# Local and pooled attention with a gated feed-forward: the leftover tokens of all batches as one block of 512, and a newly planned start

## Chip, cores and metric

The kernel runs on one core of a Trainium2 chip. Its engines work side by side, each through its own queue in order: TensorE (PE, matmuls into PSUM), VectorE (DVE), ScalarE (ACT), GpSimd (POOL) and SyncE (SP), which here only issues DMAs. The metric is device time in microseconds (us).

## What is computed

Attention over 8 batches, 8 heads, 576 tokens and 64 features per head is the sum of two parts. One lets every token see its neighbours less than 4 places away; the other averages groups of 4 tokens, attends among the 144 groups, and repeats each result 4 times. The result, 4608 tokens of 512 features, goes through a feed-forward layer with a rational function in its middle. Cut to what matters:

```python
q_d, k_d, v_d = (a.reshape(B, H, S // 4, 4, D).mean(axis=3) for a in (q, k, v))
out_up = np.repeat(sm_attn(q_d, k_d, v_d), 4, axis=2)
mask = np.abs(pos[:, None] - pos[None, :]) < 4
scores = np.where(mask, scale * np.matmul(q, k.transpose(0, 1, 3, 2)), -1e9)
out_local = np.matmul(softmax(scores), v)
x = (out_up + out_local).transpose(0, 2, 1, 3).reshape(B * S, H * D)
h = x @ w_in
P = a[0] + a[1] * h + a[2] * h**2 + a[3] * h**3
Q = 1.0 + abs(b[0]) * abs(h) + abs(b[1]) * h**2
out = (P / (Q + 1e-6)) @ w_out
```

`w_in` is 512 × 2048 and `w_out` 2048 × 512, both given in 64-bit floats.

## The kernel before

**Blocks and steps.** The feed-forward goes over blocks of tokens. The first 512 tokens of a batch are a block; the last 64 tokens (`REST`) of four batches together are a block of 256. `block_plan` orders them 0, 1, 2, R, 3, 4, 5, 6, R', 7. A step fills one PSUM bank of 512 columns with hidden values: one slice of 128 hidden features for a block of 512, two for a block of 256 (`fg`). So a block of 512 has 16 steps, one of 256 has 8: 144 in all. `h_part` issues a step's first product (L695 for block 0, L707 after it), `middle` the rational function on ACT (L720) and DVE (L735 to L771), and `o_part` the second product (L802), two steps behind, into banks 4 to 7.

**Split operands.** From block 1 on, x, the weights and the middle's result are split in a rounded part and a remainder, and a product is three matmuls (`PROD`). `split_x` splits x in place; `weights` turns a chunk of 64-bit weights into 32-bit words (L334 on ACT, L337 and L340 on DVE) and `parts` splits them (L354 on ACT, L357 on DVE). Block 0 uses the unsplit w_in and x.

**Attention.** Four pairs of heads make a batch. Of a pair, PE computes scores (L413, L423) and pooled scores (L440), DVE takes maxima (L455, L485), ACT exponentials (L470, L496), DVE normalizes (L521 for batch 0's pooled part, L531; ACT at L513 for other batches), PE transposes (L544, L551), ACT copies back (L557, L567, L568), PE applies the weights to v (L594, L582), and `put_x` (L626) adds both parts into x. Batch 0 pools q and k on DVE (L401); the others by accumulating DMAs of POOL (L390). The attention of a batch is issued into the steps of the block before it; batch 0's has nothing to run beside, and which PSUM banks its four pairs use is listed in `FIRST`: banks of the scores, of the pooled scores, of the transposes, and of the result.

**Order.** All work is entered as tasks with a cost and, for some, a due time; `Plan.run` sorts them: every engine takes the task that is ready and due earliest, and the program is written out in that order. The constants at the file's end (`H0`, `PARTS_EARLY`, `COEF`, `HOLD`...) shape the due times. The plan's times decide order only; on the chip each engine waits for semaphores.

**Fillers.** In the gaps that the plan leaves on PE at the start, `warm` issues matmuls on constants into bank 7 (L924), whose result nobody reads. They are placed up to the first task of step 0.

Of the kernel before, what the change touches and what calls it, by code (L numbers as in the profile page):

```python
# [182 lines left out]
def attention_moe(  # L183
# [123 lines left out]
    add("DVE", 0.2, lambda: nc.vector.tensor_copy(out=identb.ap, in_=ident.ap), (ident,), (identb,))  # L307
    add("SP", 0.5, lambda: nc.sync.dma_start(out=maskb.ap, in_=mask), (), (maskb,), load=0.5)

# [42 lines left out]
    def parts(w, f, due=None):  # L352
        hi, lo, word = high[w][f], low[w][f], bits[w][f]
        add("ACT", 0.5, lambda: nc.scalar.copy(out=hi.ap, in_=word.ap.bitcast(F32)), (lo,), (hi,), due=due)  # L354
# [19 lines left out]
    def load_qk(c, at=0.0):  # L374
        s, b, i = c.slot, c.b, c.i
        add("SP", 1.46, lambda: nc.sync.dma_start(out=s.qk.ap, in_=qk[b, i]), (), (s.qk,), load=1.46, at=at)

    def load_vw(c, at=0.0, due=None):
        s, b, i = c.slot, c.b, c.i
        add("SP", 0.82, lambda: nc.sync.dma_start(out=s.vw.ap, in_=vw[b, i]), (), (s.vw,), load=0.82, at=at, due=due)  # L380

# [23 lines left out]
    def scores(c, bk):  # L405
# [23 lines left out]

        add("PE", 1.01, issue, (s.qk, identb, maskb), bk)  # L430

    def scores_pooled(cs, bk):
        def issue():
            for i in range(NQ):
                for c, x in zip(cs, bk):
                    pq = flat(c.slot.pq.ap)
                    for j in range(2):
                        js = slice(j * D, (j + 1) * D)
                        o = c.pos(j) * D
                        nc.tensor.matmul(  # L440
                            x.ap[o : o + D, i * SD : (i + 1) * SD],
                            lhsT=pq[js, i * QC : i * QC + D],
                            rhs=pq[js, SD:],
                            start=True, stop=True, skip_group_check=True,
                        )

        add("PE", 1.02, issue, [c.slot.pq for c in cs], bk)

# [55 lines left out]
    def normalize(c):  # L504
# [12 lines left out]

        if c.b in EP_DVE:
            add(
# [17 lines left out]
    def turned(c, bk):  # L537
# [28 lines left out]
        add("PE", 0.11, lambda: turn_local(4, t1.ap[:, NQ * P :]), (s.el, ident), (t1,))  # L566
        add("ACT", 0.49, lambda: nc.scalar.copy(out=s.et.ap[:, :4, :], in_=tp.ap.rearrange("p (c k) -> p c k", k=P)), (tp,), (s.et,))  # L567
        add("ACT", 0.16, lambda: nc.scalar.copy(out=s.et.ap[:, 4, :], in_=t1.ap[:, NQ * P :]), (t1,), (s.et,))  # L568
# [4 lines left out]
    def weighted(cs, bk, due):  # L573
# [38 lines left out]
        def put_x(c, bank, at, lo, hi, cost):  # L612
# [7 lines left out]
            else:  # L620
                xf, r0 = xsf[2][1], c.b % 4 * REST
                dst = xf.ap[:, c.i, r0 : r0 + REST]
                room = part(xf, None, 4 * (c.i * 4 * REST + r0), 4 * REST)
            add(
# [11 lines left out]
        for c, x in zip(cs, avb):  # L636
# [30 lines left out]
    def split_x(k):  # L667
# [3 lines left out]
        for c in range(NCC):  # L671
            hi, lo = (part(x, x.ap[:, c, :], 4 * c * t, 4 * t) for x in blk.x)
            x = xsf[blk.slot][1].ap[:, c, :]
            add("ACT", 0.11 + t / 1390, lambda hi=hi, x=x: nc.scalar.copy(out=hi.ap, in_=x), (lo,), (hi,), due=due)
            add(
# [46 lines left out]
    def middle(n):  # L722
# [120 lines left out]
    for r in range(POOL):  # L843
        v = vf[r // 2]
        if r % 2:
            add(
                "POOL", 0.93, lambda r=r, v=v: nc.gpsimd.dma_start(out=v.ap, in_=vp[0, r], accum_op=ALU.add),
                (v,), (v,), load=1.3,
            )
        else:  # L850
            add("SP", 0.8, lambda r=r, v=v: nc.sync.dma_start(out=v.ap, in_=vp[0, r]), (), (v,), load=0.8)
    for c in c0:
# [37 lines left out]

    attend(1)
    for n in range(NS + LAG):
        if n < NS:
            k, s = steps[n]
# [9 lines left out]
        if o >= 0:  # L904
# [5 lines left out]
            if s == blocks[k].nstep - 1:  # L910
                store(k)

                if blocks[k].b is None and blocks[k - 1].b + 2 < B:
                    attend(blocks[k - 1].b + 2)
                elif blocks[k].b is not None and blocks[k].b + 2 < B and blocks[k + 1].b is not None:
                    attend(blocks[k].b + 2)
        if n < NS:
# [4 lines left out]
    def warm(n):  # L922
        for _ in range(n):
            nc.tensor.matmul(banks[7].ap[:, : 2 * P], lhsT=identb.ap, rhs=flat(maskb.ap)[:, : 2 * P], start=True, stop=True)  # L924
# [35 lines left out]
FIRST = (  # L960
# [70 lines left out]
```

## Time and profile before

| | |
|---|---|
| median of 3 runs | 983.53 us (983.12 to 984.9) |
| the profiled execution | 985.16 us, of which the span from first to last instruction is 983.4 |
| busy: PE, DVE, ACT, POOL | 961.4, 836.5, 811.8, 147.5 us |
| mean granted clock of PE | 0.991 |
| L802, one matmul of 512 columns | 402 ns (wh), 391 (wl) |
| chain that ended last | PE 88%, ACT 7%, DMA 2% of the span |

A matmul's duration overlaps that of the next, so a step's time is read from the chain of work or from a window, not from durations. The views used below are: the windows (busy time of each engine in a stretch of the span, with the count of instructions, the granted clock, the busy share of the DMA engines and GB/s), the chain of work that ended last (start, length, what), the timeline (start, length, engine, line, operation, count, and in brackets how long the engine had been idle and what ended it), the groups by line, and the waits. SPq is SP issuing a DMA; x9 means nine instructions merged into one row.

### The profile page before, as it was taken

To read this page: it belongs to the slowest core of one execution; us is meant where nothing else is said; L and a number is where in the kernel's file an instruction comes from. 1 tells how busy PE (TensorE), PEld (TensorE's weight loads), DVE (VectorE), ACT (ScalarE), POOL (GpSimd) and SP (SyncE) were. 2 spreads that over 40 slices of the span, in tenths; PEclk is the share of its full clock that TensorE was granted. 3 is DMA by queue.
4 is the path that set the end of the run, shared out by engine and by line. 5 is a ranking of instruction groups with operands and counts; after the bars stand their busy time and mean duration, and the time that the engine had idled before them with its cause. 6 is when DMAs were issued, how large, how long until landed. Compare 5 with 4: busy or idle time off the path is not lost.

```text
span 983.4 us, 19740 instructions
## 1 busy us (share of the span) xinstructions
PE 961.4 (98%) x7343; PEld 759.8 (77%) x7343; DVE 836.5 (85%) x1472; ACT 811.8 (83%) x2078; POOL 147.5 (15%) x176
## 2 busy tenths in 40 slices
PE   6999999999999999999999999999999999999997
PEld 4655667778788788988888787878788788898886
DVE  5889999988888888888878887988798888888886
ACT  5789999978889797679797979798888979767775
POOL 1032303031312222002222031303030220000000
PEclk9989999999999999999999999999999999999999
DMA  9577665142333333013333243424242320100001
GB/s 294 192 216 211 166 186 102 68 76 75 64 104 74 77 75 94 1 47 72 78 74 95 72 78 75 76 95 87 69 87 87 65 49 1 44 1 22 1 1 43
DMA packets 46359, 83.43 MB, mean 85 GB/s; under 512 B 6552, under 2 KB 29080, under 8 KB 46264
## 3 DMA queue, kind: packets, MB, share of 16 engines
q1 hardware_dynamic: 25912, 63.00, 19.4%
q0 software_dynamic: 20352, 19.19, 14.1%
q8 instruction: 58, 0.95, 0.4%
q14 instruction: 37, 0.30, 0.1%
HBM read 72.72 MB, written 9.44 MB: 84 GB/s over the span
## 4 chain that ended last, share of the span: by engine, by line
PE 88%; ACT 7%; DMA 2%; DVE 1%; issue 1%; SPq 0%; ACTq 0%; DVEq 0%
PE psum L802 38%; PE psum L707 36%; PE psum L582 2%; PE psum L695 2%; PE psum L594 2%; ACT m L720 2%; PE psum L551 2%; PE psum L544 2%; PE psum L423 1%; PE psum L440 1%; ACT el L470 1%; DMA qk<-in_qk_dram 1%; DMA sl<-in_w_out_dram 1%; ACT gb L720 1%; ACT sl L334 1%
## 5 line engine op out<-in xcount | busy, mean ns | idle before, releaser
L802 PE MATMUL psum<-wh,g 128*128 128x512 f32 x1152 | 369.5, 402 | 0.5 <-issue 0.4
L720 ACT ACTIVATE m<-psum,cf 128x512 f32<-128x512 f32 x288 | 218.0, 757 | 63.1 <-PE psum L707 58.2
L707 PE MATMUL psum<-xs,wh 128*128 128x512 f32 (+1 forms) x1152 | 267.3, 370 | 1.4 <-ACT gb L720 1.4
L802 PEld LDWEIGHTS psum<-wh,g 128*128 128x128 f32 x1152 | 209.4, 188 | 50.1 <-issue 5.5
L707 PEld LDWEIGHTS psum<-xs,wh 128*128 128x128 f32 x1152 | 199.0, 189 | 38.3 <-ACT gb L720 2.0
L802 PE MATMUL psum<-wl,g 128*128 128x512 f32 x576 | 224.5, 391 | 0.0
L720 ACT ACTIVATE gb<-psum,cf 128x512 f32<-128x512 f32 x144 | 116.2, 807 | 55.6 <-PE psum L802 55.6
L390 POOL DMA_DIRECT2D pq<-in_qkp_dram x84 | 73.6, 910 | 485.3 <-DMA pq<-in_qkp_dram 453.5
L707 PE MATMUL psum<-xs,wl 128*128 128x512 f32 (+1 forms) x576 | 142.7, 370 | 0.0
L762 DVE TENSOR_TENSOR g<-m,m 128x512 fp32r<-128x512 f32 x144 | 99.3, 690 | 47.7 <-ACT m L720 46.0
L802 PEld LDWEIGHTS psum<-wl,g 128*128 128x128 f32 x576 | 108.1, 188 | 23.7
L735 DVE SCALAR_TENSOR_TENSOR m<-m,cf,m 128x512 f32<-128x512 f32 x144 | 107.4, 746 | 15.7 <-ACT m L720 15.1
L741 DVE TENSOR_TENSOR m<-m,gb 128x512 f32<-128x512 f32 x144 | 99.1, 688 | 24.0 <-ACT gb L720 20.9
L707 PEld LDWEIGHTS psum<-xs,wl 128*128 128x128 f32 x576 | 100.5, 189 | 18.6 <-issue 1.2
L470 ACT ACTIVATE el<-psum,nm 128x64 f32<-128x64 f32 x320 | 97.3, 348 | 17.6 <-DVE nm L462 17.6
L720 ACT ACTIVATE gb<-m,cf 128x512 f32<-128x512 f32 x144 | 107.9, 749 | 0.7 <-DVE m L735 0.7
L765 DVE SCALAR_TENSOR_TENSOR m<-m,g 128x512 f32<-128x512 f32 x144 | 99.3, 689 | 3.3
L770 DVE TENSOR_TENSOR m<-m,m 128x512 f32<-128x512 f32 x144 | 99.1, 688 | 2.3
L740 DVE TENSOR_TENSOR m<-m,m 128x512 f32<-128x512 f32 x144 | 98.5, 684 | 1.9 <-ACT m L720 1.9
L771 DVE TENSOR_TENSOR g<-m,m 128x512 fp32r<-128x512 f32 x144 | 98.0, 681 | 0.8
L720 ACT ACTIVATE m<-gb 128x512 f32<-128x512 f32 x144 | 93.6, 650 | 3.0
L390 POOL DMA_DIRECT2D vp<-in_vp_dram x84 | 72.3, 945 | 153.9 <-DMA vp<-in_vp_dram 146.8
(63 smaller groups left out, 994.0 us busy)
## 6 DMA issues: line engine op xcount, KB each, us to landing
qk<-in_qk_dram SPq DMA_DIRECT2D x32, 590.0 KB, 6.5
pq<-in_qkp_dram POOLq DMA_DIRECT2D x84, 144.0 KB, 3.3
vw<-in_vw_dram SPq DMA_DIRECT2D x32, 320.0 KB, 3.8
out_dram<-xf SPq DMA_DIRECT2D x32, 256.0 KB, 2.0
sl<-in_w_out_dram SPq DMA_DIRECT2D x15, 512.0 KB, 4.6
sl<-in_w_in_dram SPq DMA_DIRECT2D x12, 512.0 KB, 4.8
vp<-in_vp_dram POOLq DMA_DIRECT2D x84, 72.0 KB, 3.0
pq<-in_qkp_dram SPq DMA_DIRECT2D x28, 144.0 KB, 2.2
```

The lines of the kernel that those rows point to most:

```text
L390: lambda d=dst, x=src, r=r: nc.gpsimd.dma_start(out=d.ap, in_=x[b, r, :, i], accum_op=ALU.add),
L470: nc.scalar.activation(out=s.el.ap[:, k, c.pos(j), :], in_=view[:, j, k, :], func=AF.Exp, bias=nm[:, 5 * j + k : 5 * j + k + 1], scale=sca ...
L707: nc.tensor.matmul(ph.ap[:, f * t : (f + 1) * t], lhsT=(high, low)[j][0][fc].ap[:, c, :], rhs=blk.x[i].ap[:, c, :], start=(part_ == 0 and ...
L720: add("ACT", cost, lambda: nc.scalar.activation(out=out_.ap, in_=in_, func=func, **kw), (room_in, cf, *more), (out_,))
L735: lambda: v.scalar_tensor_tensor(out=tb.ap, in0=tq.ap, scalar=b1, in1=tb.ap, op0=ALU.mult, op1=ALU.add),
L740: add("DVE", 0.61, lambda: v.tensor_tensor(out=ta.ap, in0=ta.ap, in1=tq.ap, op=ALU.mult), (ta, tq), (ta,))
L741: add("DVE", 0.61, lambda: v.tensor_tensor(out=ta.ap, in0=ta.ap, in1=u.ap, op=ALU.add), (ta, u), (ta,))
L762: add("DVE", 0.61, lambda: v.tensor_tensor(out=gh.ap, in0=ta.ap, in1=tq.ap, op=ALU.mult), (ta, tq), (gh,))
L765: lambda: v.scalar_tensor_tensor(out=tb.ap, in0=tb.ap, scalar=CONE, in1=gh.ap.bitcast(F32), op0=ALU.add, op1=ALU.mult),
L770: add("DVE", 0.61, lambda: v.tensor_tensor(out=tb.ap, in0=ta.ap, in1=tb.ap, op=ALU.subtract), (ta, tb), (tb,))
L771: add("DVE", 0.61, lambda: v.tensor_tensor(out=gl.ap, in0=tb.ap, in1=tq.ap, op=ALU.mult), (tb, tq), (gl,))
L802: nc.tensor.matmul(ob[sub].ap, lhsT=g[i].ap[:, f0 : f0 + P], rhs=flat((high, low)[j][1][fc].ap), start=(fc == 0 and m == 0), stop=(fc == N ...
```

## The change

The last 64 tokens of all eight batches become one block of 512, after block 7. Their x is collected in a buffer `xr` of its own and split from there into the buffers of slot 0, where before it was split in place. Around it the start is planned anew: the mask's load has a due time that puts it first; the loads of batch 0 are entered at a higher cost; `attend(1)` is entered after step 3 instead of ahead of all steps; pooled normalization runs on DVE for pair 2 alone instead of all four of batch 0; pair 0's transposed weights are copied by DVE; the splits of w_in for block 1 fall due 17.87 us later (`PARTS_EARLY`); banks in `FIRST` are others. Fillers are 192 columns wide in columns 320 to 511 of bank 7, denser, and go on to 62 us of the plan. `H_FIRST_BANKS` names the banks 2 and 3 for the first two steps, which they had before.

```diff
 def block_plan():
-    plan = []
-    for b in range(B):
-        plan.append(Block([(b, 0, FULL)]))
-        if b % 4 == 3:
-            plan.insert(-1, Block([(bb, FULL, REST) for bb in range(b - 3, b + 1)]))
-    return plan
+    return [Block([(b, 0, FULL)]) for b in range(B)] + [Block([(b, FULL, REST) for b in range(B)])]
...
+    xr = put("xr", [P, NCC, B * REST], F32)
...
-    add("SP", 0.5, lambda: nc.sync.dma_start(out=maskb.ap, in_=mask), (), (maskb,), load=0.5)
+    add("SP", 0.5, lambda: nc.sync.dma_start(out=maskb.ap, in_=mask), (), (maskb,), due=MASK, load=0.5)
...
+        cost = 1.46 if b else 1.9
+        add("SP", cost, lambda: nc.sync.dma_start(out=s.qk.ap, in_=qk[b, i]), (), (s.qk,), load=cost, at=at)
...
-        if c.b in EP_DVE:
+        if c.p in EP_DVE:
...
+        if c.p in ET_DVE:
+            add("DVE", 0.6, lambda: nc.vector.tensor_copy(out=s.et.ap[:, :4, :], in_=src), (tp,), (s.et,))
+        else:
+            add("ACT", 0.47, lambda: nc.scalar.copy(out=s.et.ap[:, :4, :], in_=src), (tp,), (s.et,))
...
-                xf, r0 = xsf[2][1], c.b % 4 * REST
-                dst = xf.ap[:, c.i, r0 : r0 + REST]
...
+                r0 = c.b * REST
+                dst = xr.ap[:, c.i, r0 : r0 + REST]
...
-        blk.slot = 2 if blk.b is None else blk.b % 2
+        blk.slot = (B if blk.b is None else blk.b) % 2
...
+            src = xsf[blk.slot][1] if blk.b is not None else xr
...
-    attend(1)
     for n in range(NS + LAG):
+        if n == 4:
+            attend(1)
...
-            nc.tensor.matmul(banks[7].ap[:, : 2 * P], lhsT=identb.ap, rhs=flat(maskb.ap)[:, : 2 * P], start=True, stop=True)
...
-    pe = [t for t in todo if t.engine == "PE" and t.start < due_h(0) + 5.0]
+            nc.tensor.matmul(
+                banks[7].ap[:, 320:], lhsT=identb.ap, rhs=flat(maskb.ap)[:, :192],
+                start=True, stop=True, skip_group_check=True,
+            )
...
-        n = int(WARM * (t.start - end) / 0.107)
+        n = int(WARM * (t.start - end) / 0.081)
         if n > 0:
             after[t] = n
         end = t.end
-        if t.due is not None and t.due == due_h(0):
+        if t.start > WARM_UNTIL:
             break
...
-PARTS_EARLY = 14.42
+PARTS_EARLY = -3.45
...
-COEF = 16.26
-HOLD = 0.7
-HOLD_MARGIN = 2.06
-HOLD_UNTIL = 54.4
-WARM = 0.6
+COEF = 24.82
+HOLD = 0.59
+HOLD_MARGIN = 2.63
+HOLD_UNTIL = 51.11
+H_FIRST_BANKS = (2, 3)
+WARM = 0.7
+WARM_UNTIL = 62.0
...
-    ((1, 2), 5, (2, 6, 7), (6, 7)),
-    ((3, 4), 3, (5, 3, 4), (3, 7)),
-    ((0, 1), 1, (1, 0, 6), (1, 7)),
-    ((3, 4), 0, (0, 5, 7), (4, 1)),
+    ((5, 6), 3, (2, 5, 3), (3, 5)),
+    ((0, 1), 6, (2, 5, 6), (5, 6)),
+    ((0, 1), 4, (1, 2, 0), (5, 6)),
+    ((3, 4), 3, (2, 1, 4), (0, 6)),
...
-EP_DVE = (0,)
+EP_DVE = (2,)
+ET_DVE = (0,)
+MASK = -52.93
```

More of the change, by code (lines that the diff above doesn't have):

```diff
@@ L353, in parts @@
         hi, lo, word = high[w][f], low[w][f], bits[w][f]
-        add("ACT", 0.5, lambda: nc.scalar.copy(out=hi.ap, in_=word.ap.bitcast(F32)), (lo,), (hi,), due=due)
+        add("ACT", 0.51, lambda: nc.scalar.copy(out=hi.ap, in_=word.ap.bitcast(F32)), (lo,), (hi,), due=due)
         add(
@@ L375, in load_qk @@
         s, b, i = c.slot, c.b, c.i
-        add("SP", 1.46, lambda: nc.sync.dma_start(out=s.qk.ap, in_=qk[b, i]), (), (s.qk,), load=1.46, at=at)
+        cost = 1.46 if b else 1.9
+        add("SP", cost, lambda: nc.sync.dma_start(out=s.qk.ap, in_=qk[b, i]), (), (s.qk,), load=cost, at=at)
     def load_vw(c, at=0.0, due=None):
         s, b, i = c.slot, c.b, c.i
-        add("SP", 0.82, lambda: nc.sync.dma_start(out=s.vw.ap, in_=vw[b, i]), (), (s.vw,), load=0.82, at=at, due=due)
+        cost = 0.82 if b else 0.95
+        add("SP", cost, lambda: nc.sync.dma_start(out=s.vw.ap, in_=vw[b, i]), (), (s.vw,), load=cost, at=at, due=due)
     def load_pooled(c, at=0.0):
@@ L428, in issue @@
                         )
-        add("PE", 1.01, issue, (s.qk, identb, maskb), bk)
+        add("PE", 0.99, issue, (s.qk, identb, maskb), bk)
     def scores_pooled(cs, bk):
@@ L445, in issue @@
                         )
-        add("PE", 1.02, issue, [c.slot.pq for c in cs], bk)
+        add("PE", 1.0, issue, [c.slot.pq for c in cs], bk)
     def softmax_local(c, bk):
@@ L672, in split_x @@
             hi, lo = (part(x, x.ap[:, c, :], 4 * c * t, 4 * t) for x in blk.x)
-            x = xsf[blk.slot][1].ap[:, c, :]
-            add("ACT", 0.11 + t / 1390, lambda hi=hi, x=x: nc.scalar.copy(out=hi.ap, in_=x), (lo,), (hi,), due=due)
+            src = xsf[blk.slot][1] if blk.b is not None else xr
+            src = part(src, src.ap[:, c, :], 4 * c * t, 4 * t)
+            x = src.ap
+            add("ACT", 0.14 + t / 1390, lambda hi=hi, x=x: nc.scalar.copy(out=hi.ap, in_=x), (src,), (hi,), due=due)
             add(
@@ L679, in split_x, with h_bank @@
                 ),
-                (lo, hi), (lo,), due=due,
+                (src, hi), (lo,), due=due,
             )
+    def h_bank(n):
+        return banks[H_FIRST_BANKS[n]] if n < len(H_FIRST_BANKS) else hb[n % 2]
     def h_part(n, f):
@@ L847, in attention_moe @@
                 "POOL", 0.93, lambda r=r, v=v: nc.gpsimd.dma_start(out=v.ap, in_=vp[0, r], accum_op=ALU.add),
[L848 removed]
+                (v,), (v,), load=1.9,
             )
         else:
[L851 removed]
+            add("SP", 1.4, lambda r=r, v=v: nc.sync.dma_start(out=v.ap, in_=vp[0, r]), (), (v,), load=1.4)
     for c in c0:
@@ L868, in attend @@
     def attend(b):
-        last = due_h(blocks[[blk.b for blk in blocks].index(b)].first) - SPLIT_EARLY - 3.0
-        if b % 4 == 3:
-            last = due_h(blocks[[blk.b for blk in blocks].index(b) - 1].first) - SPLIT_EARLY - 3.0
+        last = due_h(blocks[b].first) - SPLIT_EARLY - 3.0
         cs = [Pair(p) for p in range(b * NPAIR, (b + 1) * NPAIR)]
@@ L911, in attention_moe @@
                 store(k)
[L913 to L916, printed above, removed]
+                if k + 2 < B:
+                    attend(k + 2)
         if n < NS:
```

22 lines of the change are left out of this document (11 added, 11 removed).

## The prediction

> **What bounds the kernel now.** I read the windows table first: busy time by stage shows where TensorE (PE) has idle time at all.
>
> ```profile
> 0.00:58.00 58.00, 44.36 (x556) 31.23 (x556) 38.90 (x84) 37.24 (x149) 2.52 (x8) 0.88 0.71 240
> 46.00:58.00 12.00, 10.25 (x65) 5.70 (x63) 7.09 (x14) 5.43 (x12) 0.00 (x0) 0.62 0.68 243
> 46.00:54.00 8.00, 8.00 (x61) 5.11 (x60) 4.62 (x11) 2.80 (x7) 0.00 (x0) 0.50 0.70 247
> ...
> 80.00:100.00 20.00, 19.80 (x100) 11.56 (x93) 19.84 (x40) 20.00 (x64) 2.64 (x3) 1.00 0.71 221
> ...
> 735.00:840.00 105.00, 105.00 (x848) 84.49 (x847) 89.16 (x161) 90.85 (x246) 12.80 (x15) 1.00 0.22 52
> 840.00:885.00 45.00, 45.00 (x289) 41.03 (x289) 38.17 (x59) 32.78 (x53) 0.00 (x0) 1.00 0.07 24
> 885.00:972.00 87.00, 87.00 (x385) 71.78 (x383) 73.80 (x113) 62.92 (x99) 0.00 (x0) 1.00 0.03 7
> ```
>
> The columns are PE, PE's weight loads, DVE, ACT, POOL, then granted clock, DMA share and GB/s. From 735 to 972 PE has no idle time, with attention beside it (735 to 840), in the second 256-token block (840 to 885) or alone: time goes there only if PE's own work shrinks. DVE and ACT have room there. Two long windows of PE alone fill in what lies before:
>
> ```profile
> 58.00:164.40 106.40, 105.54 (x784) 1.00 0.68 175
> 164.40:375.90 211.50, 209.43 (x1654) 1.00 0.35 79
> ```
>
> So PE loses 0.9 us from 58 to 164.4 and 2.1 us to 375.9. Before 58 it idles for 13.6 us (44.36 of 58) and runs at a mean clock of 0.88. From 80 to 100 DVE (19.84 of 20) and ACT (20.00) are as full as PE: there all three bound together, and this decides how much of an earlier start is kept.
>
> **The blocks (term 1).** A step of a 256-token block in the chain of work that ended last:
>
> ```profile
> 375.90 2.87 PE psum L707 x24
> 378.78 2.75 PE psum L802 x12
> ```
>
> The number of steps stays 144 (8×16 + 2×8 before, 9×16 after). Sixteen of them, now 24 matmuls of 256 columns and 12 of 512 in 2.87 + 2.75 = 5.62 us, become 12 and 12, for which the 16 steps of 885 to 972 took 87.0 / 16 = 5.44 us: 16 × 0.18 = **2.9 us less**, on PE's uncovered path. The columns streamed are the same in number; the matmuls halve. The eight split pieces of 256 columns become four of 512; ACT (32.78 of 45) and DVE (38.17 of 45) hide them in either form. Batches 3 and 7 now have no 256-token block between them and the blocks after; 735 to 840 shows that a block with attention beside it runs without a gap, so I cost that at nothing.
>
> **The end (term 2).** The merged block is last, and each of its four result tiles leaves as two DMAs of 64 rows instead of one of 128.
>
> ```profile
> 977.52 2.05 ACT L822 COPY xf<-psum 128x512 f32<-128x512 f32 x4 [3.56 <-PE psum L802]
> 978.13 1.82 SPq L830 DMA_DIRECT2D out_dram<-xf  x4
> ...
> L830 SPq DMA_DIRECT2D out_dram<-xf x40: 332/343/594, 177.0 to 979.6; - x40
> L830 SPq EVENT_SEMAPHORE  x36: 17/17/17, 164.9 to 979.5; - x36
> ```
>
> Now SP follows the copies: four issues at a pitch of about 0.5 us, the last begun at 979.6. Eight issues at 0.343 (the median) take 2.74; with the 17 ns of a semaphore between them the last begins at about 978.13 + 7 × 0.36 = 980.65, 1.05 later; at the 0.45 pitch of SP's first loads (0.74 and 1.19, term 5) 981.3, 1.7 later. Against this each transfer is half as long, and the four together are mostly waiting for the same DMA engines. So 0 to +1.7; I take **+0.5**, nearer to the 0.36 pitch with the shorter last transfer taken off.
>
> **The clock before 58 us (term 3).** PE's timeline, then pieces of the chain:
>
> ```profile
> 42.74 0.74 PE L544 MATMUL psum<-ident,ep 112*72 112x112 f32 x6 [1.06 <-DVE xf L626]
> ...
> 45.11 0.47 PE L551 MATMUL psum<-ident,el 128*128 128x128 f32 x1 [0.96 <-ACT ept L557]
> ...
> 29.82 1.13 PE psum L594 x16
> 30.95 1.31 PE psum L582 x40
> ...
> 45.58 1.71 PE psum L695 x2
> 47.29 2.12 PE psum L594 x16
> 49.41 2.32 PE psum L582 x40
> 51.73 3.61 PE psum L695 x4
> 55.37 1.85 ACT m L720 x3
> ...
> 132.47 3.43 PE psum L695 x8
> ```
>
> After two idle gaps of about 1 us with little but transposes between them the granted clock is 0.50 from 46 to 54 (the third window above), while the chain runs over PE. The same L594 and L582 took 1.13 and 1.31 at full clock, and an L695 takes 3.43 / 8 = 0.43. What the half clock costs: 0.85 + 0.99 + 1.01 + 1.89 = 4.7 us, all on the chain to the first middle stage. The old fillers stop here: they are placed only up to the first step of the block loop in the plan. The new ones go on to 62 us of plan, in columns 320 to 511 of bank 7, which no other work of the front touches. Fillers of the same plan gaps are denser: 0.7 / 0.081 = 8.6 per us of gap of 192 columns, against 0.6 / 0.107 = 5.6 of 256. A filler ahead of work that comes sooner than planned delays it, so of 4.7 I take **-3.9**; the ends are 0 (the clock falls as now) and -4.7.
>
> The Trainium skill, page "TensorE: Matmul & The Clock Gate", section "Why this matters for your kernels", asks for no idle gap of more than about 3 us; by that rule these gaps of 1 us would not cost the clock, and fillers in them would change nothing here. The trace disagrees (0.50 after gaps of 1.06 and 0.96 us). The same page's Part 4 says that transposes do not count as PE being busy, which would join the two gaps into one; with it the fillers help.
>
> **The old fillers' own delay (term 4).**
>
> ```profile
> 21.66 2.88 PE psum L924 x13
> ...
> 24.69 0.59 ACT L567 COPY et<-psum 128x512 f32<-128x512 f32 x1 [1.60 <-PE psum L551]
> ...
> PE psum L924 <- ACT ept L557: 2.2, 1, 2.2
> ```
>
> Thirteen fillers waited 2.2 us for ACT to leave bank 7 (FIRST gives bank 7 to transposes), the clock fell, and they took 2.88 us, 0.22 each, ahead of transposes that ACT waited for. In the new FIRST no pair uses bank 7: this wait goes. What is late next is the in-order work of the other pairs on ACT and DVE. Fillers stay in front of real work, and are denser: bounds -2.9 (all of it goes) to +2 (as much again elsewhere); I take **-1.0**.
>
> **The newly placed front (term 5).**
>
> ```profile
> 0.74 0.39 SPq L376 DMA_DIRECT2D qk<-in_qk_dram  x1
> 1.19 0.42 SPq L308 DMA_DIRECT2D maskb<-in_mask_dram  x1
> ...
> 6.94 0.48 PE L413 MATMUL psum<-maskb,identb 64*64 64x320 bf16 x4
> ...
> 13.58 1.35 DVE L401 TENSOR_REDUCE pq<-qk 128x288 f32<-128x1152 f32 x1 [1.38 <-DMA qk<-in_qk_dram]
> 14.85 0.60 DVE L485 TENSOR_REDUCE nm<-psum 128x3 f32<-128x432 f32 x1
> ...
> L513 ACT ACTIVATE ep<-ep,sm 128x144 f32<-128x144 f32 x84 | 28.5, 506 | 0.0
> L521 DVE TENSOR_TENSOR ep<-ep,sm 128x432 f32<-128x432 f32 x4 | 2.4, 608 | 0.1
> ```
>
> The mask goes ahead of the first qk: that load starts 0.45 later, but fillers no longer run into the first scores, which began at 6.94 only; worth up to -1.9. The plan now counts the first batch's loads dearer (1.9 for 1.46); in the old order DVE stood at 13.58 in front of a load while L485 behind it was ready: up to -2.7 (1.38 + 1.35). Against it: for pairs 0, 1 and 3 the pooled weights are scaled on ACT, 3 × 0.506 = 1.52, in place of 0.608 on DVE: +0.9 on each pair's chain, 4.6 more on ACT and 1.8 less on DVE; the copy of pair 0 goes the other way. ACT's room (5.43 busy of the 12 us from 46 to 58) hides some of it, and where that is gone the last pair's 0.9 shows. The later coefficient load is needed first by the middle stage and hides behind attention. Which of these the new order realises, the trace of before can't show: bounds +3 (three such scalings exposed) to -4; I take **-0.6**.
>
> **Weight splits later (term 6), and what is kept.**
>
> ```profile
> 180.00:200.00 20.00, 5.83 (x9) 1.00 0.18 57
> 200.00:220.00 20.00, 0.00 (x0) 1.00 0.42 60
> ...
> 164.40:270.00 105.60, 103.53 (x804) 82.86 (x797) 95.09 (x172) 90.22 (x244) 20.03 (x24) 1.00 0.34 75
> ...
> PE psum L707 <- ACT gb L720: 1.4, 1, 1.4
> PE psum L551 <- ACT ept L557: 0.7, 1, 0.7
> ```
>
> The first two rows are L357 (the splits) on DVE alone; the third is block 1 with its five columns; the last two are all that PE waited for from 165 to 972. The w_in splits now fall due 17.9 us later, so the nine of 180 to 200 can spread over block 1, and the two waits (2.1 us) may go; I take **-0.7**, bounds -2.1 to +3 (a split that comes late holds L707 for about 0.65 each time). Terms 3 to 5 make the start 5.5 us earlier, just ahead of the stretch where DVE and ACT are full; of the 12 us from 46 to 58 they used 7.09 and 5.43, so most of what is cut was idle on them too. I keep four fifths: **+1.1** back.
>
> **Sum:** -2.9 + 0.5 - 3.9 - 1.0 - 0.6 - 0.7 + 1.1 = -7.5 us. The profiled execution took 985.16 us, 983.4 of span and 1.76 around it, and would come to 977.7; it lies 1.6 above the median of the runs, 983.53, which would come to **976.0**. I forecast that.
>
> **Rivals.**
>
> *Only the block counts.* The clock falls as now (or what the front gains is swallowed by full ACT and DVE): -2.9 + 0.5, **981.1**. For it: 19.84 and 20.00 of 20. Against it: the half clock sits on the chain, with idle time on ACT and DVE beside it. Chance 0.15, of which 0.06 lies within 0.2% of before. By the gap rule of the Trainium skill's page "TensorE: Matmul & The Clock Gate" (above) this would be the outcome.
>
> *The front comes in whole.* Terms 3 to 6 near their far ends, -4.7 - 2.9 - 2.5 - 2.1 with 0.6 given back: -14, **969.5**. For it: ACT works only 37.24 of the first 58 us. Against: all terms at once. Chance 0.12.
>
> *Splits too late.* PE waits for wl at four or so steps of block 1, 0.65 each, and the block's gain is gone with a front unchanged: **983.5**. Chance 0.08; DVE's idle 10.5 us in block 1 (95.09 of 105.6) speak against it.
>
> *Fillers in the way (slower).* At half clock a filler took 0.22: 8.6 × 0.22 = 1.9 us of filler per planned us of gap; at full clock, at 192/512 of the 2.75 / 12 = 0.229 us of an L802, it would be 0.74. If the clock stays low over the front, 0.9 us is added per us of gap; PE's idle time before 58 is 13.6 us, so up to 12 us, and it decides from about 5 us of such gaps on (4.5 against the 2.4 of terms 1 and 2). With 8: +7.2 - 2.4, **988.3**. For it: the 13 fillers at 21.66 did just that. Against: they had first waited 2.2 us, which goes. Chance 0.10.
>
> **How the numbers follow.** The forecast has 0.55; its own range is 972 to 979.5. Faster by over 0.2% (about 2 us, what a measurement of this kernel can tell from no change): 0.55 + 0.12 + 0.09 = 0.76; within: 0.06 + 0.08 = 0.14; slower: 0.10. The range 969 to 983.6 leaves out the slower rival (0.10) and about half of the best one (0.06).
>
> **What would show it.** Term 1: every step from block 1 on at 5.44, no L707 of 256 columns. Term 2: eight issues after the last copies. Term 3: clock 1.00 from 40 to 58, L594 near 1.13 throughout, middle(0) (first L720, now 55.37) near 50. Term 4: no L924 waiting for ACT. Term 5: first scores (L413) before 6.94, no DVE wait for a qk load with L485 behind it. Term 6: no PE wait in block 1, L357 seen past 200. A first L720 at 55 or later, or PE below 99% from 60 to 200, would prove the forecast wrong.

## The result and the profile after

| | before | after |
|---|---|---|
| median (lowest to highest) | 983.61 us (983.12 to 984.9, 4 runs) | 973.12 us (972.24 to 973.43, 4 runs) |
| ratio, 95% interval | | 0.989 [0.9873, 0.9907] |
| profiled execution, span | 985.16, 983.4 | 973.43, 971.6 |
| mean granted clock | 0.991 | 0.997 |

The change takes 10.5 us off, where -7.5 was forecast. The lines of the changed kernel lie a little lower: L714 is the old L707, L702 the old L695, L809 the old L802, L727 the old L720, L829 and L837 the old L822 and L830, L928 the fillers. Four marks cut a span in stages: the first ACT instruction of middle(0), the first product of block 1, the last four copies out of PSUM, and the end. All experiments below are in the same table; "ratio" is against the kernel before, run beside each on the same chip.

| kernel | to middle(0) | to block 1 | to the last copies | to the end | span | median us | ratio [95%] |
|---|---|---|---|---|---|---|---|
| before | 55.4 | 109.1 | 813.1 | 5.9 | 983.4 | 983.61 | |
| **after** | 46.8 | 107.9 | 808.4 | 8.5 | 971.6 | 973.12 | 0.989 [0.9873, 0.9907] |
| block_alone | 50.3 | 111.1 | 811.2 | 8.5 | 981.2 | 985.33 | 1.0018 [1.0002, 1.0033] |
| block_parts | 52.2 | 111.9 | 808.3 | 8.6 | 980.9 | 982.74 | 0.9987 [0.9971, 1.0003] |
| old_parts | 47.0 | 107.5 | 810.5 | 8.5 | 973.5 | 975.42 | 0.9904 [0.9877, 0.9932] |
| before_late_fillers | 51.3 | 110.1 | 813.1 | 5.8 | 980.3 | 982.9 | 0.9985 [0.9971, 1.0] |
| old_fillers | 46.2 | 108.0 | 808.4 | 8.5 | 971.2 | 974.24 | 0.9897 [0.9874, 0.9921] |
| no_fillers | 46.9 | 110.1 | 808.5 | 8.5 | 974.0 | 975.77 | 0.9922 [0.9903, 0.994] |
| no_fill_old_first | 49.8 | 111.7 | 811.3 | 8.6 | 981.4 | 983.17 | 0.9997 [0.9977, 1.0016] |
| old_mask | 48.6 | 108.8 | 808.4 | 8.6 | 974.4 | 976.26 | 0.9921 [0.9905, 0.9938] |
| old_ep | 47.7 | 109.2 | 809.0 | 8.8 | 974.7 | 976.87 | 0.9929 [0.9912, 0.9946] |
| old_costs | 46.7 | 110.1 | 808.7 | 8.6 | 974.0 | 975.78 | 0.9906 [0.9884, 0.9927] |
| one_store | 46.8 | 108.6 | 808.5 | 24.9 | 988.8 | 990.2 | 1.0061 [1.0042, 1.008] |
| interleaved | 46.6 | 109.0 | 808.4 | 6.1 | 970.1 | 970.96 | 0.9857 [0.9834, 0.9879] |

The stages are those of one profiled execution each, the medians those of all runs. The kernels ran on several chips, where the kernel before had medians of 983.61 to 984.87, and the changed kernel was not run beside every other; so a difference of about 1 us between two medians of the table says little by itself.

So the 11.8 us between the two profiled spans are -8.6 up to middle(0), -1.1 from there to block 1, -4.7 up to the last copies, and +2.6 **lost** at the end. The windows of the changed kernel show the stages (columns as in the prediction):

```profile
0.00:46.85 46.85, 41.59 (x621) 31.95 (x622) 34.09 (x76) 35.81 (x152) 2.51 (x8) 1.00 0.77 259
46.85:152.00 105.15, 103.33 (x744) 64.24 (x742) 103.74 (x197) 102.52 (x271) 27.78 (x32) 1.00 0.71 189
152.00:255.00 103.00, 103.00 (x780) 82.99 (x778) 96.30 (x174) 91.45 (x247) 19.72 (x24) 1.00 0.37 81
255.00:960.00 705.00, 704.65 (x5074) 570.09 (x5073) 599.56 (x1018) 581.38 (x1412) 96.94 (x114) 1.00 0.26 60
```

PE, DVE and ACT are all near full from 46.85 to 152, the clock is 1.00 throughout, and PE has no idle time in block 1 (third row), where before it waited 2.1 us. Its waits in the whole span, first up to 60 us, then from there to 975 (who waited for whom: us in all, times, longest):

```profile
PE psum L928 <- DMA maskb<-in_mask_dram: 3.1, 1, 3.1
PE psum L702 <- ACT gb L727: 1.6, 1, 1.6
...
PE psum L809 <- ACT xs L678: 0.3, 1, 0.3
PE psum L809 <- DVE g L778: 0.2, 1, 0.2
```

No filler waits for ACT any more, and no L714 for ACT. The chain that ended last:

```profile
39.46 5.36 DMA sl<-in_w_in_dram
44.90 0.68 ACT sl L330
45.58 0.50 ACT wh L350
46.17 0.69 ACT sl L330
46.85 1.72 ACT m L727 x3
...
941.10 2.72 PE psum L714 x12
943.82 2.72 PE psum L809 x12
...
963.07 1.07 ACT xf L829 x2
```

A step of the merged block is 12 + 12 matmuls of 512 in 5.44 us. At the front, what now stands before middle(0) is a load of w_in and ACT's conversions of it: ACT waited for data there, not for PE. The end, in the timeline:

```profile
963.07 2.05 ACT L829 COPY xf<-psum 128x512 f32<-128x512 f32 x4 [3.56 <-PE psum L809]
963.68 5.03 SPq L837 DMA_DIRECT2D out_dram<-xf  x8
```

The copies take as long as before; the eight stores keep SP for 5.03 us, where the four took 1.82.

### The profile page after: what moved, and what is told of

It reads as the page before. It is cut to its first block, busy times and chain, and to the rows that moved or that the text cites. A ratio compares the mean times of both kernels' runs of the same rounds, so it can differ in the third digit from the quotient of the medians.

```text
span 971.6 us, 19508 instructions
## 1 busy us (share of the span) xinstructions
PE 956.1 (98%) x7225; PEld 751.4 (77%) x7225; DVE 836.0 (86%) x1466; ACT 813.2 (84%) x2082; POOL 147.0 (15%) x176
## 4 chain that ended last, share of the span: by engine, by line
PE 93%; ACT 5%; DMA 1%; DVE 1%; issue 0%; ACTq 0%
PE psum L809 40%; PE psum L714 36%; PE psum L702 5%; PE psum L584 2%; PE psum L421 2%; PE psum L542 2%; PE psum L596 2%; PE psum L549 2%; PE psum L438 1%; ACT el L468 1%; ACT m L727 1%; PE psum L411 1%; ACT ep L494 1%; DMA sl<-in_w_in_dram 1%; ACT gb L727 0%
## 5 line engine op out<-in xcount | busy, mean ns | idle before, releaser
L809 PE MATMUL psum<-wh,g 128*128 128x512 f32 x1152 | 368.8, 401 | 0.5 <-ACT xs L678 0.3
L714 PE MATMUL psum<-xs,wh 128*128 128x512 f32 x1024 | 262.9, 394 | 0.0
L727 ACT ACTIVATE m<-psum,cf 128x512 f32<-128x512 f32 x288 | 218.4, 759 | 40.5 <-PE psum L714 39.5
L809 PEld LDWEIGHTS psum<-wh,g 128*128 128x128 f32 x1152 | 210.5, 188 | 50.8 <-issue 3.3
L809 PE MATMUL psum<-wl,g 128*128 128x512 f32 x576 | 224.8, 391 | 0.0
L714 PEld LDWEIGHTS psum<-xs,wh 128*128 128x128 f32 x1024 | 189.5, 188 | 39.7 <-ACT gb L727 0.2
L727 ACT ACTIVATE gb<-psum,cf 128x512 f32<-128x512 f32 x144 | 116.7, 810 | 50.7 <-PE psum L809 50.4
L714 PE MATMUL psum<-xs,wl 128*128 128x512 f32 x512 | 140.5, 396 | 0.0
L742 DVE SCALAR_TENSOR_TENSOR m<-m,cf,m 128x512 f32<-128x512 f32 x144 | 107.5, 746 | 27.5 <-ACT m L727 27.4
L809 PEld LDWEIGHTS psum<-wl,g 128*128 128x128 f32 x576 | 108.1, 188 | 23.5
L714 PEld LDWEIGHTS psum<-xs,wl 128*128 128x128 f32 x512 | 94.2, 188 | 20.6 <-issue 1.0
L727 ACT ACTIVATE gb<-m,cf 128x512 f32<-128x512 f32 x144 | 108.0, 750 | 0.9 <-DVE m L742 0.9
L727 ACT ACTIVATE m<-gb 128x512 f32<-128x512 f32 x144 | 93.5, 649 | 6.5 <-DVE m L747 3.6
```

Source lines behind the costliest of these rows:

```text
L714: nc.tensor.matmul(ph.ap[:, f * t : (f + 1) * t], lhsT=(high, low)[j][0][fc].ap[:, c, :], rhs=blk.x[i].ap[:, c, :], start=(part_ == 0 and ...
L727: add("ACT", cost, lambda: nc.scalar.activation(out=out_.ap, in_=in_, func=func, **kw), (room_in, cf, *more), (out_,))
L742: lambda: v.scalar_tensor_tensor(out=tb.ap, in0=tq.ap, scalar=b1, in1=tb.ap, op0=ALU.mult, op1=ALU.add),
L809: nc.tensor.matmul(ob[sub].ap, lhsT=g[i].ap[:, f0 : f0 + P], rhs=flat((high, low)[j][1][fc].ap), start=(fc == 0 and m == 0), stop=(fc == N ...
```

## The experiments

Three questions were open: what the end cost, whether the fillers and the clock made the start shorter, and which part of the new start did if they did not. Each kernel is sorted anew by the plan, so a difference holds the part itself and the order that follows from it.

**one_store: the end with four stores.** From the changed kernel, the two stores of a tile become one with a destination of 2 × 64 rows:

```diff
-            for i, (b, t, n) in enumerate(rows):
...
-                        out=out[b * S + t : b * S + t + n, :], in_=osb[i * n : (i + 1) * n, :]
+                b, t, n = blk.rows[2 * sub]
+                dst = out.rearrange("(b s) d -> b s d", s=S)[b : b + 2, t : t + n, :]
+                src = osb
+            add("SP", 0.7, lambda d=dst, x=src: nc.sync.dma_start(out=d, in_=x), ...)
```

> The changed kernel with each result tile of the merged block stored by one DMA (2 x 64 x 512 of the output from 128 x 512) instead of two of 64 rows. Theory (SP's issue of a 64-row store costs about 0.6 us, so eight of them set the end): the time from the first of the last four copies to the end of the span goes from 8.5 us back to about 5.9, and the whole is 2.6 us shorter than the changed kernel, 970.5. Rival (one DMA over two row groups is issued as slowly as two): no change, 973.

It took 990.2 us, and the whole loss is at the end, 24.9 us for 8.5. Its timeline and its last window:

```profile
964.47 10.01 SPq L837 DMA_DIRECT2D out_dram<-xf  x4
```

```profile
960.00:989.00 29.00, 4.36 (x18) 2.77 (x16) 2.77 (x4) 2.36 (x5) 0.00 (x0) 0.61 0.10 36
```

Fewer issues did not help: four took SP 10 us, and 1 MB needed 24 us. A DMA share of 0.10 over 29 us is 0.10 × 16 × 29 = 46 us of one engine, in 24 us of transfer: about two of the 16 engines carried everything. That is what the Trainium skill states on the page "DMA: Bandwidth & Descriptors", section "Why a DMA increments its semaphore by 16 and not by 1": the number of engines is the largest up to 16 that divides the slowest dimension that isn't 1, on the source's side and on the destination's; here the destination's is 2. The run leaves term 2 open, but tells how to try again.

**interleaved: the same four stores with 64 outermost.** The tokens of two batches are put into `xr` in turn (batch 0 token 512, batch 1 token 512, batch 0 token 513, ...), so that a tile's 128 rows leave as 64 × 2 × 512:

```diff
-                r0 = c.b * REST
-                dst = xr.ap[:, c.i, r0 : r0 + REST]
+                r0 = c.b // 2 * P
+                dst = xr.ap[:, c.i, r0 : r0 + P].rearrange("p (s two) -> p two s", two=2)[:, c.b % 2, :]
...
+                dst = out.rearrange("(b s) d -> s b d", s=S)[t : t + n, b : b + 2, :]
```

> The changed kernel with the merged block's tokens in another order, so that one DMA per result tile (64 x 2 x 512, its slowest dimension 64) stores what two stored. Theory (eight issues of 0.6 us set the end, and the store over 2 x 64 rows was slow only because two of the 16 DMA engines carried it): first of the last copies to the end of the span 5.9 us instead of 8.5, whole 2.6 us shorter than the changed kernel, near 970.5 to 971 at a ratio of 0.9865. Rival (a transfer with three dimensions is issued as slowly as two DMAs, or strided writes of x delay the attention): 973 or more.

970.96 us, the fastest of all: the end is 6.1 us again. Timeline and a window of it:

```profile
964.02 2.05 ACT L829 COPY xf<-psum 128x512 f32<-128x512 f32 x4 [3.56 <-PE psum L809]
964.63 2.61 SPq L836 DMA_DIRECT2D out_dram<-xf  x4
```

```profile
966.00:970.00 4.00, 0.00 (x0) 0.00 (x0) 0.00 (x0) 0.08 (x1) 0.00 (x0) 0.85 0.69 259
```

The DMA engines are busy to 0.69, not 0.10. So the 2.4 us between 8.5 and 6.1 are the price of eight issues in place of four, and of nothing else in the merged block. The kernel before had stores of 64 rows too, in its first block of 256, where the timeline gives them:

```profile
431.71 2.46 SPq L830 DMA_DIRECT2D out_dram<-xf  x4
```

Four in 2.46 us are 0.6 each. At that, the eighth begins 7 × 0.63 = 4.4 us after the first (5.03 / 8 = 0.63 in the changed kernel). The single issues (shortest, median and longest in ns), first those four, then the four of interleaved:

```profile
L830 SPq DMA_DIRECT2D out_dram<-xf x4: 550/565/587, 431.7 to 433.6; - x4
```

```profile
L836 SPq DMA_DIRECT2D out_dram<-xf x4: 547/562/666, 964.6 to 966.7; - x4
```

A store of 64 × 2 × 512 is issued no faster than one of 64 rows; the four last stores of the kernel before, of 128 rows each, took 338 to 352 ns. What interleaved saves is four issues, not the length of one.

**old_fillers: the changed kernel with the fillers of before.** 256 columns wide, sparser, and only up to the first task of step 0:

```diff
-                banks[7].ap[:, 320:], lhsT=identb.ap, rhs=flat(maskb.ap)[:, :192],
-                start=True, stop=True, skip_group_check=True,
+                banks[7].ap[:, : 2 * P], lhsT=identb.ap, rhs=flat(maskb.ap)[:, : 2 * P],
+                start=True, stop=True,
...
-        n = int(WARM * (t.start - end) / 0.081)
+        n = int(WARM * (t.start - end) / 0.107)
...
-        if t.start > WARM_UNTIL:
+        if t.due is not None and t.due == due_h(0):
-WARM = 0.7
+WARM = 0.6
```

> The changed kernel with the old fillers: 256 columns from column 0 of bank 7, 0.6 of the gap at 0.107 each, and none past the first step of the block loop. Theory that the clock made the gain (term 3, 3.9 us): granted clock falls to 0.5 between 38 and 52, first middle stage near 50.5, 977. Rival (the new order of the start made it, and it leaves no gap in which the clock falls): clock stays at 1.0 but for a few us, first middle stage near 47, 973 to 974.

974.24 us: within 0.2% of the changed kernel, and its marks are the same to about 0.5 us. Two of its windows:

```profile
44.00:50.00 6.00, 3.23 (x8) 1.25 (x7) 5.37 (x10) 5.11 (x10) 0.26 (x1) 1.00 0.97 377
50.00:56.00 6.00, 6.00 (x60) 3.50 (x59) 5.91 (x11) 6.00 (x12) 3.25 (x4) 1.00 1.06 338
```

Without a filler there PE was idle for 2.8 of the six us from 44 to 50, and the clock stayed at 1.00. The late, dense fillers did not make the gain.

**before_late_fillers: the same from the other side.** The kernel before, its order untouched, with fillers of its own kind up to 50 us of plan, from 28.7 on in bank 6:

```diff
-    pe = [t for t in todo if t.engine == "PE" and t.start < due_h(0) + 5.0]
+    pe = [t for t in todo if t.engine == "PE" and t.start < 50.0]
...
-        if t.due is not None and t.due == due_h(0):
-            break
```

> The kernel before with its fillers (256 columns, 0.6 of the gap) going on past the first step of the block loop up to 50 us of plan, there in bank 6; order and blocks unchanged. Theory (the half clock from 46 to 54 costs 4.7 us and fillers hold it off): clock 1.0 there, first middle stage near 51 instead of 55.4, 979.5. Rival (plan gaps are not where the hardware's gaps are, so the clock falls all the same): 983.5.

982.9 us (10 runs) against 984.07 (23 runs): -1.2, and the interval ends at 1.0. Its windows:

```profile
14.00:20.00 6.00, 5.86 (x76) 4.40 (x73) 5.52 (x13) 4.53 (x30) 0.00 (x0) 0.72 1.06 305
20.00:26.00 6.00, 4.10 (x24) 3.19 (x24) 2.71 (x5) 3.94 (x21) 0.00 (x0) 0.72 1.03 389
26.00:42.00 16.00, 15.65 (x244) 11.07 (x244) 14.01 (x33) 14.95 (x56) 0.00 (x0) 1.00 0.47 177
42.00:54.00 12.00, 10.64 (x120) 6.88 (x117) 11.30 (x25) 8.65 (x19) 0.00 (x0) 1.00 0.67 215
```

The half clock of 46 to 54 is gone and middle(0) comes at 51.3 instead of 55.4, yet the median gains only 1.2. So the profiled execution of before seems to have drawn a bad clock there which most runs do not have. block_alone (below) keeps the old fillers, banks and constants, and has the full clock in the very window in which the kernel before had 0.50, with middle(0) at 50.3; so has block_parts, with 52.2:

```profile
46.00:54.00 8.00, 6.16 (x65) 3.56 (x62) 7.49 (x15) 5.97 (x11) 0.00 (x0) 1.00 0.85 271
```

Of the 8.6 us up to middle(0) between the two profiles, 3 to 5 would then be this draw, an estimate from 50.3 to 52.2 in place of 55.4. The runs of the kernel before point the same way: the 23 have spans of 979.3 to 985.4 and mean clocks of 0.991 to 0.998, with a correlation of -0.76 and 0.72 us less for each 0.001 more. The page "TensorE: Matmul & The Clock Gate" of the Trainium skill, Part 1, section "What's actually happening", says that the clock is judged over a window that runs freely, so that the same kernel turns cold and warm at other places from run to run; these runs agree.

**no_fillers and no_fill_old_first: the start without any cover.** The changed kernel with `WARM = 0.0`, once with its own banks and once with those of before:

```diff
-    ((5, 6), 3, (2, 5, 3), (3, 5)),
-    ((0, 1), 6, (2, 5, 6), (5, 6)),
-    ((0, 1), 4, (1, 2, 0), (5, 6)),
-    ((3, 4), 3, (2, 1, 4), (0, 6)),
+    ((1, 2), 5, (2, 6, 7), (6, 7)),
+    ((3, 4), 3, (5, 3, 4), (3, 7)),
+    ((0, 1), 1, (1, 0, 6), (1, 7)),
+    ((3, 4), 0, (0, 5, 7), (4, 1)),
```

> The changed kernel without any filler. Theory (the new order is what shortens the start, and fillers only keep the clock from falling in it now and then): granted clock falls in the first 20 us and perhaps around 46, first middle stage 47 to 51, 974 to 978. Rival (fillers are needed throughout): clock 0.5 over most of the start, first middle stage past 52, 980 or more.

> The changed kernel without any filler and with the old banks of FIRST. Theory (with realistic load costs the plan finds a short start with either set of banks, within 1 us): as the kernel without fillers. Rival (the new banks make the start): first middle stage 2 us or more later than without fillers alone, and the time with it.

no_fillers: 975.77, so all fillers together are worth 2.6 us by the medians (the two intervals just overlap), and none of it before middle(0), which comes at 46.9, beside 46.8 with them. The loss is behind it, in the clock:

```profile
14.00:26.00 12.00, 8.51 (x177) 6.56 (x172) 9.16 (x24) 11.14 (x56) 0.00 (x0) 1.00 1.04 356
...
44.00:50.00 6.00, 2.52 (x6) 1.07 (x5) 4.15 (x9) 4.85 (x8) 0.07 (x1) 0.93 1.01 373
50.00:56.00 6.00, 6.00 (x53) 2.65 (x52) 5.42 (x9) 4.80 (x8) 3.44 (x4) 0.78 1.05 339
```

The same eight matmuls of L702 take 1.6 us more in the chain for it, first in the changed kernel, then in no_fillers; the stage from middle(0) to block 1 is 2.2 longer:

```profile
49.30 3.70 PE psum L702 x8
```

```profile
49.42 5.28 PE psum L702 x8
```

no_fill_old_first: 983.17 (the median of nine runs; a tenth took 2420), the time of the kernel before. The old banks, with the order that the plan makes of them, cost 7.4 us more than the new ones, with no filler in either: 3.0 up to middle(0), 1.6 from there to block 1, and 2.8 in block 1 and behind, where PE waits for 2.5 us in place of 0.6. In its windows and its timeline:

```profile
14.00:26.00 12.00, 9.65 (x96) 7.50 (x92) 6.38 (x15) 10.15 (x50) 0.00 (x0) 0.64 1.03 353
...
50.00:62.00 12.00, 9.61 (x61) 4.94 (x62) 9.03 (x16) 9.63 (x19) 4.40 (x5) 0.72 1.04 332
```

```profile
12.66 0.58 PE L438 MATMUL psum<-pq 64*64 64x144 f32 x6 [2.87 <-ACT el L468]
```

The pooled scores wait 2.87 us for ACT's exponentials to leave their bank; after that wait the clock is 0.64 from 14 to 26, where the new banks, with as little PE work there, keep 1.00. The new banks do not take the wait away: there the same row waits 1.26 us at 11.15, and 1.09 once more at 28.55. Over the first 60 us, with the new banks and then with the old:

```profile
PE psum L438 <- ACT el L468: 2.4, 2, 1.3
```

```profile
PE psum L438 <- ACT el L468: 2.9, 1, 2.9
```

Banks and clock go together here. The mean clock is 0.989 in the median of the nine runs and 0.9925 in that of no_fillers' four; at 0.50 us for each 0.001 (the 13 runs of the kernel before beside these) or the 0.72 above that is, as an estimate, 1.8 to 2.5 of the 7.4 us. That the longer wait is what lowered the clock is not shown, and which waits make up the rest was not followed through.

**old_mask, old_ep, old_costs: the other parts of the start, each put back alone.**

```diff
-    add("SP", 0.5, lambda: nc.sync.dma_start(out=maskb.ap, in_=mask), (), (maskb,), due=MASK, load=0.5)
+    add("SP", 0.5, lambda: nc.sync.dma_start(out=maskb.ap, in_=mask), (), (maskb,), load=0.5)
```

```diff
-EP_DVE = (2,)
-ET_DVE = (0,)
+EP_DVE = (0, 1, 2, 3)
+ET_DVE = ()
```

```diff
-        cost = 1.46 if b else 1.9
+        cost = 1.46
-        cost = 0.82 if b else 0.95
+        cost = 0.82
...
-                (v,), (v,), load=1.9,
+                (v,), (v,), load=1.3,
-            add("SP", 1.4, lambda r=r, v=v: nc.sync.dma_start(out=v.ap, in_=vp[0, r]), (), (v,), load=1.4)
+            add("SP", 0.8, lambda r=r, v=v: nc.sync.dma_start(out=v.ap, in_=vp[0, r]), (), (v,), load=0.8)
```

> The changed kernel with the mask loaded after the first qk, as before. Theory (the first scores wait for the mask and for fillers behind it; mask first brings them from 6.9 to 6.05): first scores 0.5 to 1 us later, first middle stage 0.5 to 1 us later, 974. Rival (the first scores wait for qk, which the mask delays): 972.5 to 973.

> The changed kernel with the pooled scaling of all four pairs on DVE and pair 0's copy on ACT, as before. By the prediction's term 5 (1.52 on ACT for 0.61 on DVE, +0.9 on a pair's chain) this would be up to 0.9 us shorter at the first middle stage, 972 to 973. Rival (DVE is the fuller engine behind 46 us, and 1.8 us of work taken from it is worth more than ACT's 4.6): 974 to 975.

> The changed kernel planned with the old load costs of the first batch (qk 1.46, vw 0.82, vf 0.8 and 1.3). Theory (an order planned with loads that are cheaper than the hardware's makes DVE and ACT stand in front of loads while other work is ready): DVE waits for qk loads with ready work behind, first middle stage 2 to 4 us later than 46.8, 975 to 977. Rival (banks, mask and the place of the second batch's attention make the start): within 1 us of the changed kernel.

old_mask: 976.26, +3.1 over the changed kernel's median. The first scores start at 8.2 instead of 6.0 and ACT's first exponentials wait longer; the first row is old_mask, the second the changed kernel:

```profile
ACT el L468 <- DVE nm L460: 9.0, 1, 9.0
```

```profile
ACT el L468 <- DVE nm L460: 6.3, 1, 6.3
```

2.7 us of a late start on ACT come out at 1.9 at middle(0) and 2.7 at block 1: little of a late start is made up later. The run does not price the mask alone. In both kernels 18 fillers, which read the mask, take 3.04 us between its arrival (5.24 and 3.08) and the first scores; how much of the 3.1 would stay without them there was not tried.

old_ep: 976.87, +3.7. middle(0) is 0.9 later, block 1 is 2.2 later. Its PE waited before middle(0) for:

```profile
PE psum L542 <- ACT up L642: 1.1, 1, 1.1
PE psum L549 <- ACT ept L555: 0.9, 1, 0.9
...
PE psum L542 <- DVE ep L519: 0.4, 1, 0.4
```

The run puts back two things at once: the pooled scaling of three pairs goes to DVE, and the copy of pair 0's transposed weights to ACT. So scaling on ACT and copying on DVE are a gain together, where the prediction counted the scaling as a cost; which of the two it is, and why it is worth more than the 1.8 us that the scaling takes off DVE, these runs do not settle.

old_costs: 975.78, +2.7. middle(0) is at the same place (46.7); the loss is behind it. 13 instead of 16 matmuls of block 0's first product (L702) were done by 46.7, and block 1 starts 2.1 later. DVE waits longer for the loads of q and k, first in old_costs, then in the changed kernel:

```profile
DVE pq L399 <- DMA qk<-in_qk_dram: 7.2, 2, 4.3
```

```profile
DVE pq L399 <- DMA qk<-in_qk_dram: 4.9, 2, 3.7
```

Of these three only old_ep's interval lies clear of the changed kernel's (0.9912 against 0.9907); for old_mask and old_costs the size rests on the medians and on the marks in the traces. By the ratios old_costs loses 1.6 us rather than 2.7, and old_mask 3.0.

**block_alone, block_parts, old_parts: the block and the splits.** block_alone is the kernel before with the hunks of the merged block and of `xr`, and nothing of the new start. block_parts is block_alone, and old_parts the changed kernel, with one constant set otherwise:

```diff
 block_parts
-PARTS_EARLY = 14.42
+PARTS_EARLY = -3.45
 old_parts
-PARTS_EARLY = -3.45
+PARTS_EARLY = 14.42
```

> The kernel before with the merged block last and nothing else of the change: its constants, banks, loads and fillers are the old ones. Theory: the sixteen cheaper steps give 2.9 us and the eight stores at the end take 2.65 back, so 983.3, no change; the old start stays (first middle stage near 55). Rival (the prediction's term 2, +0.5 at the end): 981.1. Second rival (without the 256-token blocks the later attention runs into DVE or ACT): PE waits after 270 us, slower than 984.

> The merged block alone (old start and fillers) with the late splits of w_in. Theory (the block alone lost what it saved in DVE's full stretch, and late splits free DVE): PE waits from 55 to 270 fall from 4 us to under 2, and it is 2 us shorter than the block alone, 983 beside 985. Rival (the old start sets the time, splits don't matter): within 1 us of the block alone.

> The changed kernel with the splits of w_in due as early as before (PARTS_EARLY 14.42). Theory (term 6: late splits free DVE between 150 and 195, so the two PE waits of block 1, 2.1 us, went): first middle stage stays near 46.8, PE waits of 1 to 2 us come back in block 1, 975. Rival (those waits went with the earlier and denser start, not with the splits): 973.

block_alone is not faster: 985.33 (12 runs) against 984.07, ratio 1.0018 [1.0002, 1.0033]. From block 1 to the last copies it gains 1.9, and the end loses 2.6. block_parts takes 982.74, 2.6 less than block_alone, and old_parts 2.3 more than the changed kernel (1.4 by the ratios, 2.1 by the stage). PE's waits from 160 on in block_alone, and all that it waited for from 60 on in old_parts:

```profile
PE psum L705 <- ACT gb L718: 1.4, 1, 1.4
PE psum L547 <- ACT ept L553: 0.7, 1, 0.7
PE psum L800 <- ACT gb L718: 0.3, 1, 0.3
PE psum L800 <- DVE g L769: 0.2, 1, 0.2
```

```profile
PE psum L714 <- ACT gb L727: 1.4, 1, 1.4
PE psum L809 <- ACT xs L678: 0.3, 1, 0.3
PE psum L809 <- DVE g L778: 0.2, 1, 0.2
```

The 1.4 us of L707 in the kernel before (L705 and L714 here) come back wherever the early due time does, and go with the later one: block 1 to the last copies is 813.1 and 811.2 with early splits in the old front, 808.3 with late ones, 810.5 and 808.4 in the new. In old_parts the waits shown are 1.4 of the 2.1 us; the rest was not traced.

## Why the prediction came out as it did

The forecast was 976.0 with 972 to 979.5 as its own range; 973.12 lies inside. The sum was near, but only step 1 came near its price; the errors of the others partly offset one another. Steps against measurement:

| step | forecast | measured | shown by |
|---|---|---|---|
| 1 blocks | -2.9 | -1.9 to -2.9 | 5.44 us a step (-2.9); 813.1 to 808.3 in block_parts, less 2.1 of waits (-2.7); to 811.2 in block_alone (-1.9) |
| 2 end | +0.5 | +2.6 | 5.9 to 8.5; 6.1 in interleaved |
| 3 clock | -3.9 | -1.2 | before_late_fillers; mean clock 0.995 (median of before's 23 runs) to 0.997, × 0.72 us per 0.001 = 1.4 |
| 4, 5 fillers' wait, front, with what is kept | -1.0 - 0.6 + 1.1 | -6.7 | block 1 at 161.4 in before_late_fillers, 154.7 after; one execution of each |
| 6 splits | -0.7 | -2.1 | old_parts, 810.5 to 808.4 |
| sum | -7.5 | -10.2 (with -2.8 in step 1) | medians: -10.5 |

**Step 1 was right**, to the size of a step: the halved number of matmuls is worth 0.18 us for each of 16 steps, all on PE's uncovered path. With the old due time the stage gained only 1.9 of the 2.9; 0.3 of the difference is a new wait (L800 for ACT), the rest was not traced.

**Step 2 was mis-sized.** Its direction and place held, SP issuing eight stores behind the last copies. The 0.343 used for an issue was the median of a line that holds stores of 128 and of 64 rows; the maximum of 594 ns in that same quoted row belonged to those of 64. At 0.594 and 0.017 for a semaphore the last issue would begin 7 × 0.61 = 4.3 after 978.13, at 982.4, 2.8 later than the 979.6 of before, and 2.6 was measured.

**Step 3 had the wrong agent and a size from one draw.** The clock is at 1.00 from 40 to 58 as forecast, but old_fillers has it there too. The 4.7 us of half clock were true of the profiled execution and not of the kernel: over 23 runs the mean clock differs by 0.007 and the span by 6 us, and block_alone and block_parts, with the old fillers, have 1.00 in that window. The median could gain only what an average run loses, 1.0 to 1.4. What stands of the idea: without any filler the new order loses 2.6 us, of which 1.6 show in its profiled execution as matmuls at a lower clock.

**Step 4 was right in kind**: no filler waits for ACT. Its size can't be told from that of step 5, since the new banks take the wait away.

**Step 5 failed, and it is where the time came from.** The prediction said that the trace of before could not show which of the parts the new order would realise, and took -0.6 between -4 and +3, as if they cancelled. They did not cancel: each part put back alone costs 2.7 to 3.7 us by the medians, the banks 7.4 without fillers. These overlap (their sum of 17 is more than the 6.7 there is), as each undoing leaves the plan's other constants unfitted. One part came with the other sign, the scaling on ACT with the copy on DVE: the 4.6 us more on ACT were held against it, though in the prediction's own window of 46 to 58 ACT was the emptier engine (5.43 busy of 12 us, DVE 7.09), and undoing both costs 3.7. That DVE would no longer stand in front of a load came only in part: it waits 4.9 us for loads of q and k, in two waits, where it was 4.3. But the first pooled maxima now run ahead of the second wait, where before (L485) they began at 14.85; in old_costs they begin at 11.50, so most of this is not the load costs' doing:

```profile
10.35 0.60 DVE L483 TENSOR_REDUCE nm<-psum 128x3 f32<-128x432 f32 x1
```

And what the old banks cost was priced by one wait of a filler (2.2 us) alone; with no filler at all PE's own pooled scores wait 2.87 us for such a bank, and PE waits longer in block 1 and behind.

**Step 6 was right in mechanism and lay at its far bound** (-2.1): both waits went, and none came in their place, where the splits now run on into block 1 (the group of L353, the splits on DVE; first and last start before the shapes):

```profile
L353 DVE TENSOR_TENSOR wl<-wb,wh x32: 681/685/697, 36.8 to 202.8; 128x512 fp32r<-128x512 f32 x32
```

The last one starts past 200, where before there was none.

**What was to be given back was not.** The full DVE and ACT from 80 to 100 were to swallow a fifth of an earlier start. The stage from middle(0) to block 1 got shorter instead, 109.1 to 107.9, and 110.1 in before_late_fillers; there is 103.33 of PE work in the 105.15 us of the second window, so all three engines are near full and simply start earlier.

The two signs that were to prove the forecast wrong did not come: the first L727 is at 46.8, and PE is busy for 139.78 of the 140 us from 60 to 200.

Of the rivals, **"the front comes in whole"** described best what happened (969.5, with the end taken at +0.5), though with the clock as its main term, which was not it. **"Only the block counts"** fell: the block alone is worth nothing here, since nearly all of its 2.9 is lost again at the end. **"Splits too late"** and **"fillers in the way"** did not come: no wait for wl, and old and new fillers within 1.1 us of each other. The price of the second was too high in itself: it took 0.22 us, the time of a filler of 256 columns at half clock, for one of 192, which by the columns would be 0.17, so 1.4 us for each planned us of gap and not 1.9.

Open: entering `attend(1)` after step 3 and the new values of `COEF`, `HOLD` and its limits were not tried alone, nor the old banks together with the new fillers. Nor were some small changes of the plan that the full diff holds besides: `SPLIT_EARLY` 9.84 for 9.51, `PAIR_GAP` 3.65 for 3.53, and the costs of a few tasks. How the 6.7 us of steps 4 and 5 divide among the parts is therefore not known.

## What to carry to other kernels

Take a duration from the row of the same shape: a line's median over mixed shapes hid a store 1.7 times as dear, and it sat on the path's end. Before pricing a cold clock from a profile, look at the spread of clock and span over many runs; one execution shows a draw, the median loses only the average. At a start where nothing runs beside, look for who waits for a PSUM bank: placing banks so that PE waits less for the stage before was worth more there (7.4 us) than all fillers (2.6), and four stores with a dimension of 64 outermost ended 2.4 us earlier than eight.

## What the runs showed of the hardware

A store of 64 rows of 2 KB costs SP about 0.6 us to issue (565 ns in the median of the four at 431.7, 2.46 / 4 and 5.03 / 8 with what lies between two), one of 128 rows 0.34 (338 to 352 ns at the end of the kernel before), but 0.56 when its 128 rows are 64 × 2 (interleaved); a store of 256 KB whose destination is 2 × 64 × 512 runs on two of the 16 engines and takes about 6 us (24 / 4), while 64 × 2 × 512 moved at 259 GB/s. The clock of TensorE differs from run to run of the same kernel by 0.007 of its mean, worth 0.5 to 0.72 us for each 0.001 in sets of 13 and 23 runs; and it fell to 0.50 in one execution after two gaps of 1 us with little but transposes between them, while in another kernel 2.8 idle us of six left it at 1.00.
